# Attention with beacons and a max-out FFN: casts and turns of a pair two to three pairs ahead, loads held by GpSimd memsets

## The chip, the cores and the metric

The kernel runs on one core of one Trainium2 chip. The metric is the device time in microseconds; the median of three runs of the kernel before is 290.99 us (288.12, 290.99 and 295.52). The profile is of one execution. Its span counts from the first to the last instruction of the program; "the profiled run's time" is the device time of that same execution.

Engines are named as in the profile: PE is TensorE (PEld its weight loads), DVE VectorE, ACT ScalarE, POOL GpSimd, SP SyncE, which here only issues DMAs.

## The reference

For 8 batches, 8 heads, 576 tokens, 16 beacons and 64 values a head, attention over beacon keys and causal keys, and after it a feed-forward layer with the maximum of three products:

```
k_all = np.concatenate([beacon_k, k], axis=2)
v_all = np.concatenate([beacon_v, v], axis=2)
scores = scale * np.matmul(q, k_all.transpose(0, 1, 3, 2))
causal[:, Nb:] = np.triu(np.ones((S, S), dtype=bool), k=1)
a = softmax(np.where(causal, -1e9, scores))
x = matmul(a, v_all).transpose(0, 2, 1, 3).reshape(B * S, H * D)
h = np.maximum(np.maximum(x @ w1, x @ w2), x @ w3)
out = h @ w_out
```

x has 4608 rows of 512, h 4608 rows of 768. Inputs and output are float32.

## The kernel before, in words

**Tiles.** Two heads of one batch are a pair: 4 pairs a batch, 32 in all, numbered through. Two pairs are a quad. A pair's q and k come from HBM in float32 into one stage tile "st" of 96 partitions (`load_pair`, line 196), are cast to bf16 into tiles "p" (`cast_pair`, line 265) and turned, so that the head's dimension lies on the partitions, into qT and kT. Pairs from 14 on are turned by a DMA with transpose, two a pair (`cross_piece`, line 375: "turn" in this text); earlier ones by TensorE. There are 8 stage tiles (line 109), 3 buffers for each of the two cast tiles (line 110) and 6 for qT and kT (line 144). V of a batch comes in two pieces, each into a stage tile of the same kind (`load_v`, line 290), and is cast by `cast_v` (line 303) into one of 2 buffers.

**Steps.** The order of the whole program is written out by hand in two lists of steps, `first_steps` (line 897) and `loop_steps` (line 1073). Each step gives its instructions to the engines' queues, and each engine runs its own in that order. The steps that matter:

- `("scores", p, g, ...)` (line 502): the matmuls of group g (of 4) of pair p's scores, and ScalarE's exponential of them (L522).
- `("mask", p, g, "pool")` (line 528): GpSimd zeroes what the causal mask forbids (L541).
- `("values", quad, half, ...)` (line 560): sums and weighted values on TensorE (L582), some 120 small matmuls for the two halves of a quad. "invert" and "multiply" put 1/sum on them (L603, L605, L615) and write x into xT; "cross x" (line 671) copies a part of xT for the other half of TensorE's array.
- `("unit", place)` (line 688): 16 matmuls of x with one of the three weights (L699), and DVE's running maximum (L629, L631). There are 126 units; 18 make one batch's share.
- `("out", n, place)` (line 717): n tiles of h @ w_out (L725); `("store", 1)` sends them out from SP (line 759).
- `("cast", p, "pool", "pool")`: both casts of pair p on GpSimd (L259). `("cross", p, 0)` and `("cross", p, 1)`: the two turns, issued by SP (L378). `("keys", p, "act")`: the beacons' columns of kT (L459).
- `("load", n, gate)` takes the next n loads from the list `loads` (lines 772 to 775) and issues them on SP (L211 for pairs, L276 and L279 for V). With a gate of "pool" or "dve" that engine first writes one column of the stage tile (line 202) or one value (line 294), so that the DMA waits until this engine has come to that place in its own queue. Without a gate the DMA starts as soon as SP reaches it and the tile is free.

SP is one queue: loads, turns and stores leave in the order of the steps.

In a batch of the loop (18 units) stand the scores of 4 pairs, two values steps, four or five tiles of the output, and the casts, turns and loads for later pairs. Below, "unit n" is a place: n units stand before it.

Of the kernel before, what the change touches and what calls it, by code (L numbers as in the profile page):

```python
# [16 lines left out]
def kernel(  # L17
# [15 lines left out]
    B, H, S, D = q.shape  # L33
# [24 lines left out]
    PPB = H // 2  # L58
    PPQ = PPB // n_quad
    NPAIR = B * PPB  # L60
    RING = 3

    B_PE = 4
# [70 lines left out]
    bk32 = const.tile([NB_DMA, H, D], FP32, name="bk32")  # L134
# [43 lines left out]
    def L(fn, *a):  # L178
        return lambda *more: fn(*a, *more)
# [656 lines left out]
    def start_late():  # L836
# [224 lines left out]
        ("load", 1, "pool"),  # L1061
        ("scores", 7, 3, 0),
        ("load", 1),
# [57 lines left out]
        ("cast", 12, "pool", "pool"),  # L1121
        ("load", 1),
        ("load", 1),
        ("scores", 9, 3, 0, 3),
        ("mask", 9, 3, "pool"),
        ("unit", 1),
        ("scores", 9, 1, 0, 0),
        ("mask", 9, 1, "pool"),
        ("unit", 2),
        ("cast", 13, "pool", "pool"),  # L1130
        ("unit", 3),
# [14 lines left out]
        ("cast", 14, "pool", "pool"),  # L1146
        ("cross", 14, 0),
        ("cross", 14, 1),
        ("load", 1),
        ("unit", 2),  # L1150
# [6 lines left out]
        ("cast keys 2", "pool"),  # L1157
        ("load", 1),
# [3 lines left out]
        ("cross keys",),  # L1162
        ("scores", 11, 2, 0, 0),
        ("mask", 11, 2, "pool"),
        ("unit", 1),
        ("scores", 11, 3, 0, 2),
# [4 lines left out]
        ("unit", 1),  # L1171
        ("unit", 2),
        ("cast", 15, "pool", "pool"),
        ("cross", 15, 0),
        ("cross", 15, 1),
        ("load", 1),
# [9 lines left out]
        ("cast", 16, "pool", "pool"),  # L1186
        ("cross", 16, 0),
        ("cross", 16, 1),
        ("load", 1),
# [13 lines left out]
        ("load", 1),  # L1203
        ("cast v", 3, 0, "pool"),
# [3 lines left out]
        ("keys", 14, "act"),  # L1208
# [3 lines left out]
        ("cast v", 3, 1, "pool"),  # L1212
# [6 lines left out]
        ("cast", 17, "pool", "pool"),  # L1219
        ("cross", 17, 0),  # L1220
        ("cross", 17, 1),
        ("load", 1),
# [3 lines left out]
        ("keys", 15, "act"),  # L1226
        ("scores", 13, 3, 0, 3),
        ("mask", 13, 3, "pool"),
        ("unit", 0),
        ("scores", 13, 1, 0, 1),  # L1230
# [5 lines left out]
        ("cast", 18, "pool", "pool"),  # L1236
        ("cross", 18, 0),
        ("cross", 18, 1),
        ("load", 1),
# [3 lines left out]
        ("keys", 16, "act"),  # L1243
# [11 lines left out]
        ("unit", 3),  # L1255
        ("scores", 14, 1, 0, 2),
        ("mask", 14, 1, "pool"),
        ("unit", 0),
        ("cast", 19, "pool", "pool"),
        ("cross", 19, 0),  # L1260
        ("cross", 19, 1),
        ("load", 1),
# [3 lines left out]
        ("keys", 17, "act"),  # L1266
        ("scores", 15, 2, 0, 2),
        ("mask", 15, 2, "pool"),
        ("unit", 0),
        ("scores", 15, 3, 0, 1),  # L1270
# [5 lines left out]
        ("load", 1, "pool"),  # L1276
# [9 lines left out]
        ("cast", 20, "pool", "pool"),  # L1286
        ("cross", 20, 0),
        ("cross", 20, 1),
        ("load", 1),
# [7 lines left out]
        ("load", 1),  # L1297
        ("cast v", 4, 0, "pool"),
# [3 lines left out]
        ("keys", 18, "act"),  # L1302
# [3 lines left out]
        ("cast v", 4, 1, "pool"),  # L1306
# [6 lines left out]
        ("cast", 21, "pool", "pool"),  # L1313
        ("cross", 21, 0),
        ("cross", 21, 1),
        ("load", 1),
# [13 lines left out]
        ("cast", 22, "pool", "pool"),  # L1330
        ("cross", 22, 0),
        ("cross", 22, 1),
        ("load", 1),
# [3 lines left out]
        ("keys", 20, "act"),  # L1337
# [11 lines left out]
        ("unit", 1),  # L1349
        ("scores", 18, 1, 0, 3),  # L1350
        ("mask", 18, 1, "pool"),
        ("unit", 2),
        ("cast", 23, "pool", "pool"),
        ("cross", 23, 0),
        ("cross", 23, 1),
        ("load", 1),
# [3 lines left out]
        ("keys", 21, "act"),  # L1360
        ("scores", 19, 2, 0, 3),
        ("mask", 19, 2, "pool"),
        ("unit", 2),
        ("scores", 19, 3, 0, 0),
# [5 lines left out]
        ("load", 1, "pool"),  # L1370
# [9 lines left out]
        ("cast", 24, "pool", "pool"),  # L1380
        ("cross", 24, 0),
        ("cross", 24, 1),
        ("load", 1),
# [9 lines left out]
        ("load", 1),  # L1393
        ("cast v", 5, 0, "pool"),
# [3 lines left out]
        ("keys", 22, "act"),  # L1398
# [3 lines left out]
        ("cast v", 5, 1, "pool"),  # L1402
# [6 lines left out]
        ("cast", 25, "pool", "pool"),  # L1409
        ("cross", 25, 0),  # L1410
        ("cross", 25, 1),
        ("load", 1),
# [3 lines left out]
        ("keys", 23, "act"),  # L1416
        ("scores", 21, 3, 0, 3),
        ("mask", 21, 3, "pool"),
        ("unit", 2),
        ("scores", 21, 1, 0, 0),  # L1420
# [5 lines left out]
        ("cast", 26, "pool", "pool"),  # L1426
        ("cross", 26, 0),
        ("cross", 26, 1),
        ("load", 1),
# [3 lines left out]
        ("keys", 24, "act"),  # L1433
# [11 lines left out]
        ("unit", 3),  # L1445
        ("scores", 22, 1, 0, 1),
        ("mask", 22, 1, "pool"),
        ("unit", 2),
        ("cast", 27, "pool", "pool"),
        ("cross", 27, 0),  # L1450
        ("cross", 27, 1),
        ("load", 1),
# [3 lines left out]
        ("keys", 25, "act"),  # L1456
        ("scores", 23, 2, 0, 1),
        ("mask", 23, 2, "pool"),
        ("unit", 2),
        ("scores", 23, 3, 0, 0),  # L1460
# [5 lines left out]
        ("load", 1, "pool"),  # L1466
# [9 lines left out]
        ("cast", 28, "pool", "pool"),  # L1476
        ("cross", 28, 0),
        ("cross", 28, 1),
        ("load", 1),
# [7 lines left out]
        ("load", 1),  # L1487
        ("cast v", 6, 0, "pool"),
# [3 lines left out]
        ("keys", 26, "act"),  # L1492
# [3 lines left out]
        ("cast v", 6, 1, "pool"),  # L1496
# [6 lines left out]
        ("cast", 29, "pool", "pool"),  # L1503
        ("cross", 29, 0),
        ("cross", 29, 1),
        ("load", 1),
# [3 lines left out]
        ("keys", 27, "act"),  # L1510
        ("scores", 25, 3, 0, 0),
        ("mask", 25, 3, "pool"),
        ("unit", 1),
        ("scores", 25, 1, 0, 2),
# [5 lines left out]
        ("cast", 30, "pool", "pool"),  # L1520
        ("cross", 30, 0),
        ("cross", 30, 1),
# [3 lines left out]
        ("keys", 28, "act"),  # L1526
# [11 lines left out]
        ("unit", 0),  # L1538
        ("scores", 26, 1, 0, 3),
        ("mask", 26, 1, "pool"),  # L1540
        ("unit", 1),
        ("cast", 31, "pool", "pool"),
        ("cross", 31, 0),
        ("cross", 31, 1),
# [3 lines left out]
        ("keys", 29, "act"),  # L1548
# [17 lines left out]
        ("cross x", 5, 1, 1, "pool"),  # L1566
        ("out", 2, 1),
# [8 lines left out]
        ("cast v", 7, 0, "pool"),  # L1576
# [3 lines left out]
        ("keys", 30, "act"),  # L1580
# [3 lines left out]
        ("cast v", 7, 1, "pool"),  # L1584
# [5 lines left out]
        ("unit", 1),  # L1590
        ("scores", 29, 2, 0, 2),
        ("mask", 29, 2, "pool"),
        ("unit", 0),
        ("keys", 31, "act"),
        ("scores", 29, 3, 0, 3),
        ("mask", 29, 3, "pool"),
        ("unit", 1),
        ("scores", 29, 1, 0, 2),
# [4 lines left out]
        ("unit", 1),  # L1603
        ("scores", 30, 2, 0, 2),
# [106 lines left out]
```

## Time and profile before

| | |
|---|---|
| runs | 288.12, 290.99, 295.52 us; median 290.99 |
| profiled run's own time | 288.71 us |
| its span | 286.9 us |
| granted clock of TensorE | 1.00 |
| moved by DMA | 46.27 MB, 161 GB/s on average |
| SP's queue (q1) | 111888 packets, 39.20 MB |
| instructions' queue (q8) | 40 packets, 0.66 MB |

The program has three stretches: the start up to 57 us, in which the first batches are computed as their data come in; the loop, from "late" at some 57 us to the last scores at some 250 us; and the end, which has only units and output tiles. A row of the table by stretches gives for each engine its busy time and its number of instructions, then the granted clock, the share of the DMA engines' time and GB/s. A row of the timeline has the start, the length, the engine and line, and in square brackets the idle time before it with what ended it. For DMAs on SP the length is the time that SP needed to issue it, not the transfer.

### The profile page before, as it was taken

Reading aid. Unit: us, or ns where it says so; the run is one execution under the profiler, and the core shown is the slowest. Engines: PE = TensorE matmul, PEld = TensorE weight load, DVE = VectorE, ACT = ScalarE, POOL = GpSimd, SP = SyncE. Lnnn points to the kernel's source line nnn. Section 1 sums busy time; section 2 is a strip of 40 time slices with the busy share of each in tenths; the row PEclk is TensorE's granted clock in tenths of the full one; section 3 lists DMA queues with packets and bytes.
Section 4 is the critical chain, followed back from the end, with each engine's and each line's share of the span. In section 5 each row is a group of like instructions: output and inputs, shape, how many; then the busy total and the mean of one; then the engine's idle time right before and its main releaser. Section 6 shows DMA issues by size and latency. Waiting matters only on the chain.

```text
span 286.9 us, 11693 instructions
## 1 busy us (share of the span) xinstructions
PE 275.5 (96%) x5099; PEld 204.3 (71%) x5099; DVE 177.1 (62%) x331; ACT 155.1 (54%) x249; POOL 140.6 (49%) x280
## 2 busy tenths in 40 slices
PE   7999999899899999999999998989999999999995
PEld 6656777667677577876888476866888478867762
DVE  2455878866566665756666565645666565761654
ACT  3886676877363367734765176624765186624000
POOL 4562228898763187626763396616763173400000
PEclk9999999999999999999999999999999999999999
DMA  9999999989999989889999999899999220003004
GB/s 156 177 166 210 219 238 159 244 198 218 231 185 159 148 167 305 133 156 177 192 218 163 158 162 295 138 185 164 242 214 141 78 110 5 2 3 148 2 2 183
DMA packets 118307, 46.27 MB, mean 161 GB/s; under 512 B 107248, under 2 KB 112880, under 8 KB 118256
## 3 DMA queue, kind: packets, MB, share of 16 engines
q1 hardware_dynamic: 111888, 39.20, 72.8%
q0 software_dynamic: 5808, 6.00, 13.3%
q8 instruction: 40, 0.66, 1.1%
q10 hardware_dynamic: 560, 0.33, 0.4%
q14 instruction: 11, 0.09, 0.1%
HBM read 35.13 MB, written 9.44 MB: 155 GB/s over the span
## 4 chain that ended last, share of the span: by engine, by line
PE 87%; DMA 4%; ACT 3%; issue 2%; POOL 1%; DVE 1%; ACTq 0%; POOLq 0%
PE t L699 44%; PE t L725 16%; PE t L582 11%; PE t L513 6%; DMA quad<-in_k_dram 2%; ACT at_sb L522 2%; PE pv L637 2%; DMA bk<-in_beacon_k_dram 2%; PE sc L513 1%; PE sc L637 1%; PE fps L637 1%; PE t L397 1%; POOL at_sb L541 1%; PE wide L582 1%; PE pv L582 1%
## 5 line engine op out<-in xcount | busy, mean ns | idle before, releaser
L699 PE MATMUL t<-xT,w_sb 64*128 64x288 bf16 (+1 forms) x1008 | 130.5, 285 | 0.9 <-issue 0.9
L699 PE MATMUL t<-xC,wC 64*128 64x288 bf16 (+1 forms) x1008 | 130.3, 285 | 0.0
L522 ACT ACTIVATE at_sb<-t 128x992 bf16<-128x992 f32 (+1 forms) x96 | 82.7, 863 | 54.4 <-PE t L513 46.4
L541 POOL TENSOR_SCALAR_AFFINE_SELECT at_sb<-at_sb 128x256 bf16<-128x256 bf16 (+2 forms) x143 | 53.3, 389 | 61.2 <-ACT at_sb L522 46.4
L631 DVE TENSOR_TENSOR hT<-hT,t 128x576 bf16<-128x576 bf16 (+1 forms) x84 | 63.7, 762 | 31.3 <-PE t L699 31.3
L699 PEld LDWEIGHTS <-w_sb 64*128 64x128 bf16 x1008 | 52.7, 94 | 12.8 <-issue 2.1
L699 PEld LDWEIGHTS <-wC 64*128 64x128 bf16 x1008 | 52.7, 94 | 11.3
L725 PE MATMUL t<-w_out_sb,hT 128*128 128x512 bf16 x210 | 46.9, 380 | 0.0
L259 POOL CAST p<-st 96x768 bf16<-96x768 f32 x44 | 35.0, 822 | 8.0 <-DMA qT<-p 7.4
L629 DVE CAST hT<-t 128x576 bf16<-128x576 f32 (+1 forms) x36 | 27.7, 769 | 15.2 <-PE t L699 15.0
L615 DVE TENSOR_TENSOR xT<-t,recip 128x288 bf16<-128x288 f32 (+2 forms) x78 | 23.0, 351 | 22.6 <-ACT recip L605 18.9
L725 PEld LDWEIGHTS <-hT 128*128 128x128 bf16 x210 | 19.9, 98 | 23.3 <-issue 0.2
L680 POOL COPY xC<-xT 64x576 bf16<-64x576 bf16 (+1 forms) x26 | 18.2, 699 | 36.1 <-DVE xT L615 35.9
L513 PE MATMUL t<-qT,kT 64*128 64x288 bf16 (+4 forms) x288 | 33.4, 279 | 0.0
L733 DVE COPY y<-t 128x1024 f32<-128x1024 f32 (+1 forms) x20 | 21.8, 1090 | 17.1 <-PE t L725 16.8
L582 PEld LDWEIGHTS <-v_sb 128*32 128x32 bf16 (+1 forms) x1408 | 24.8, 96 | 5.4 <-issue 4.2
L582 PE MATMUL t<-at_sb,v_sb 128*32 128x96 bf16 (+8 forms) x1144 | 24.0, 228 | 3.2 <-issue 3.2
L513 PEld LDWEIGHTS <-kT 64*128 64x128 bf16 x400 | 18.8, 94 | 10.7 <-issue 6.3
L603 ACT ACTIVATE lnd<-t 128x288 f32<-128x288 f32 x26 | 10.7, 410 | 28.7 <-PE t L582 28.7
L522 ACT ACTIVATE at_sb<-sc 128x736 bf16<-128x736 f32 (+5 forms) x28 | 23.2, 862 | 4.3 <-PE sc L513 4.1
L315 POOL CAST v_sb<-st 128x1536 bf16<-128x1536 f32 (+2 forms) x21 | 18.4, 894 | 0.0
L637 PEld LDWEIGHTS <-w_sb 128*128 128x128 bf16 x144 | 13.1, 98 | 3.3 <-issue 1.4
(125 smaller groups left out, 214.2 us busy)
## 6 DMA issues: line engine op xcount, KB each, us to landing
out_dram<-y SPq DMA_DIRECT2D x15, 512.0 KB, 5.3
st<-in_q_dram SPq DMA_DIRECT2D x24, 288.0 KB, 5.8
st<-in_k_dram SPq DMA_DIRECT2D x24, 288.0 KB, 6.6
st<-in_v_dram SPq DMA_DIRECT2D x24, 256.0 KB, 5.4
w_sb<-in_moe_w_dram POOLq DMA_DIRECT2D x6, 384.0 KB, 8.4
st<-in_v_dram SPq DMA_DIRECT2D x8, 224.0 KB, 4.9
st<-in_v_dram SPq DMA_DIRECT2D x8, 160.0 KB, 5.2
out_dram<-y SPq DMA_DIRECT2D x5, 256.0 KB, 2.7
```

Of the source, the lines that this page charges most:

```text
L259: cast(t16.rearrange("p r h d -> p h r d"), st[0:QP, i * NQ2 : (i + 1) * NQ2].rearrange("p (h r d) -> p h r d", h=2, r=QR),)
L513: nc.tensor.matmul(ps[:, e, off : off + q1 - q0], kT[hs, 128 * t : 128 * t + 128], qT[hs, q0:q1], start=True, stop=True, tile_position=(64 ...
L522: nc.scalar.activation(out=both_heads(p, gi), in_=ps[:, :, 0 : g_width(p, gi)], func=AF.Exp, scale=scale)
L541: nc.gpsimd.affine_select(out=view, in_=view, compare_op=ALU.is_ge, fill=0.0, base=x0, pattern=[[0, 2], [1, hi - lo]], channel_multiplier=-1,)
L582: nc.tensor.matmul(ps[bank][32 * j : 32 * j + 32, lo + q0 - qa : lo + qb - qa], lhsT, at_view(PPQ * quad + j // 2, t, j % 2, q0, qb), star ...
L615: nc.vector.tensor_mul(xT[:, 2 * g + part - 1, c0 + ca : c0 + cb], ps[bank][:, lo : lo + cb - ca], recip[:, ca:cb],)
L629: (by_i or by_dve)(h, ps)
L631: nc.vector.tensor_max(h, h, ps)
L637: nc.tensor.matmul(ps[:, f], w_in[i][:, ct, 128 * (ft + f) : 128 * (ft + f + 1)], xT[:, ct, lo : lo + MID], start=(ct == 0), stop=(ct == n ...
L699: nc.tensor.matmul(ps[:, e], w[own(e), ct, cols], x, start=(ct == 0 and not over), stop=(ct == n_ct - 1 and over), tile_position=(64 * e, 0),)
L725: nc.tensor.matmul(ps[:, u], h_tile(tt + u, ft), w_out_sb[:, ft, :], start=(ft == 0), stop=(ft == n_ft - 1),)
L733: nc.vector.tensor_copy(y[:, 0:n], ps[:, 0:n])
```

## The change

Three things. The list of loads gets another order: the beacons' keys and then, batch by batch, V and the four pairs of the batch after it (before, the pairs came one earlier). Casts, turns and keys of a pair stand later among the steps, so that a pair is turned two to three pairs ahead of its scores instead of four. And the loads, some of which stood together, are spread over the batch, most of them with a memset on GpSimd as gate; the others follow the turns of the same place and have none. The prologue loses two loads (pairs 14 and 15), which move into the loop. Scores, masks, units, values, "out" and "store" keep their order among each other.

Where the steps stand for one batch and for the loads around it ("unit" as above; the same distances return in each batch):

| | before | after |
|---|---|---|
| load of pairs 14, 15 | prologue (gate POOL, none) | units 1, 5 (both POOL) |
| load of V of batch 3, two pieces | 4, 9 (no gates) | 9, 13 (POOL) |
| load of pairs 16, 17, 18, 19 | 4, 12, 17, 18 (no gates) | 16 POOL, 18 none, 20 none, 24 POOL |
| load of V of batch 4 | 23, 27 (no gates) | 27, 30 (POOL) |
| load of pair 20 | 19 (no gate) | 33 (POOL) |
| cast and turns of 14, 15, 16, 17 | 9, 17, 18, 23 | 18, 20, 27, 31 |
| cast and turns of 18, 19, 20, 21 | 27, 31, 36, 41 | 36, 38, 45, 49 |
| first scores of 18, 19, 20, 21 | 44, 49, 54, 58 | the same |
| casts of V of batch 4 | 37, 39 | 41, 43 |

The diff, cut to its core (one batch, from unit 36 on; the other batches are changed alike):

```
-    loads += [L(load_beacons, B_PE, B, bk32)] + load_pairs(16, 17)
+    loads.append(L(load_beacons, B_PE, B, bk32))
     for b in range(3, B):
-        loads += load_v_pieces(b) + load_pairs(PPB * b + 5, min(PPB * b + 9, NPAIR))
+        loads += load_v_pieces(b) + load_pairs(PPB * (b + 1), min(PPB * (b + 2), NPAIR))
...
-        ("load", 1, "pool"),
         ("scores", 7, 3, 0),
-        ("load", 1),
...
         ("cross x", 2, 1, 1, "pool"),
-        ("cast", 20, "pool", "pool"),
-        ("cross", 20, 0),
-        ("cross", 20, 1),
-        ("load", 1),
+        ("cast", 18, "pool", "pool"),
+        ("cross", 18, 0),
+        ("cross", 18, 1),
+        ("load", 1, None),
         ("out", 2, 0),
         ("store", 1),
         ("out", 2, 1),
         ("store", 1),
         ("scores", 16, 0, 0, 3),
         ("mask", 16, 0, "pool"),
         ("unit", 2),
-        ("load", 1),
-        ("cast v", 4, 0, "pool"),
         ("scores", 16, 2, 0, 0),
         ("mask", 16, 2, "pool"),
         ("unit", 3),
-        ("keys", 18, "act"),
+        ("cast", 19, "pool", "pool"),
+        ("cross", 19, 0),
+        ("cross", 19, 1),
+        ("load", 1, None),
+        ("keys", 17, "act"),
         ("scores", 16, 3, 0, 1),
         ("mask", 16, 3, "pool"),
         ("unit", 2),
-        ("cast v", 4, 1, "pool"),
         ("scores", 16, 1, 0, 0),
         ("mask", 16, 1, "pool"),
         ("unit", 3),
         ("scores", 17, 0, 0, 1),
         ("mask", 17, 0, "pool"),
         ("unit", 2),
-        ("cast", 21, "pool", "pool"),
-        ("cross", 21, 0),
-        ("cross", 21, 1),
-        ("load", 1),
+        ("cast v", 4, 0, "pool"),
         ("scores", 17, 2, 0, 0),
         ("mask", 17, 2, "pool"),
         ("unit", 3),
-        ("keys", 19, "act"),
+        ("load", 1, "pool"),
+        ("keys", 18, "act"),
         ("scores", 17, 3, 0, 1),
         ("mask", 17, 3, "pool"),
         ("unit", 2),
+        ("cast v", 4, 1, "pool"),
         ("scores", 17, 1, 0, 0),
         ("mask", 17, 1, "pool"),
         ("unit", 3),
         ("scores", 18, 0, 0, 1),
         ("mask", 18, 0, "pool"),
         ("unit", 2),
-        ("cast", 22, "pool", "pool"),
-        ("cross", 22, 0),
-        ("cross", 22, 1),
-        ("load", 1),
+        ("cast", 20, "pool", "pool"),
+        ("cross", 20, 0),
+        ("cross", 20, 1),
+        ("load", 1, "pool"),
+        ("keys", 19, "act"),
```

More of the change, by code (lines that the diff above doesn't have):

```diff
@@ L1126 @@
         ("unit", 1),
+        ("cast", 12, "pool", "pool"),
+        ("load", 1, "pool"),
         ("scores", 9, 1, 0, 0),
@@ L1129 @@
         ("unit", 2),
+        ("unit", 3),
         ("cast", 13, "pool", "pool"),
-        ("unit", 3),
         ("scores", 10, 0, 0, 1),
@@ L1145 @@
         ("unit", 0),
-        ("cast", 14, "pool", "pool"),
-        ("cross", 14, 0),
-        ("cross", 14, 1),
         ("load", 1),
+        ("load", 1, "pool"),
         ("unit", 2),
@@ L1161 @@
         ("unit", 3),
-        ("cross keys",),
+        ("load", 1, "pool"),
         ("scores", 11, 2, 0, 0),
@@ L1165 @@
         ("unit", 1),
+        ("cast keys 2", "pool"),
         ("scores", 11, 3, 0, 2),
@@ L1171 @@
         ("unit", 1),
+        ("load", 1, "pool"),
         ("unit", 2),
[L1173 to L1176, printed above, removed]
+        ("cross keys",),
         ("unit", 3),
@@ L1185 @@
         ("cross x", 1, 1, 1, "pool"),
[L1186 to L1189, printed above, removed]
+        ("cast", 14, "pool", "pool"),
+        ("cross", 14, 0),
+        ("cross", 14, 1),
+        ("load", 1, None),
         ("pair", 12, "act", "dve", 2),
@@ L1207 @@
         ("unit", 2),
-        ("keys", 14, "act"),
+        ("cast", 15, "pool", "pool"),
+        ("cross", 15, 0),
+        ("cross", 15, 1),
+        ("load", 1, None),
         ("scores", 12, 3, 0, 3),
@@ L1218 @@
         ("unit", 0),
[L1219 to L1222, printed above, removed]
+        ("cast v", 3, 0, "pool"),
         ("scores", 13, 2, 0, 1),
@@ L1225 @@
         ("unit", 2),
-        ("keys", 15, "act"),
+        ("load", 1, "pool"),
+        ("keys", 14, "act"),
         ("scores", 13, 3, 0, 3),
@@ L1229 @@
         ("unit", 0),
+        ("cast v", 3, 1, "pool"),
         ("scores", 13, 1, 0, 1),
@@ L1235 @@
         ("unit", 0),
[L1236 to L1239, printed above, removed]
+        ("cast", 16, "pool", "pool"),
+        ("cross", 16, 0),
+        ("cross", 16, 1),
+        ("load", 1, "pool"),
+        ("keys", 15, "act"),
         ("scores", 14, 2, 0, 1),
@@ L1255 @@
         ("unit", 3),
+        ("load", 1, "pool"),
         ("scores", 14, 1, 0, 2),
@@ L1258 @@
         ("unit", 0),
[L1259 to L1262, printed above, removed]
+        ("cast", 17, "pool", "pool"),
+        ("cross", 17, 0),
+        ("cross", 17, 1),
         ("scores", 15, 0, 0, 1),
@@ L1269 @@
         ("unit", 0),
+        ("load", 1, "pool"),
         ("scores", 15, 3, 0, 1),
@@ L1275 @@
         ("unit", 0),
-        ("load", 1, "pool"),
         ("unit", 1),
@@ L1301 @@
         ("unit", 3),
-        ("keys", 18, "act"),
+        ("cast", 19, "pool", "pool"),
+        ("cross", 19, 0),
+        ("cross", 19, 1),
+        ("load", 1, None),
+        ("keys", 17, "act"),
         ("scores", 16, 3, 0, 1),
@@ L1319 @@
         ("unit", 3),
-        ("keys", 19, "act"),
+        ("load", 1, "pool"),
+        ("keys", 18, "act"),
         ("scores", 17, 3, 0, 1),
@@ L1349 @@
         ("unit", 1),
+        ("load", 1, "pool"),
         ("scores", 18, 1, 0, 3),
@@ L1352 @@
         ("unit", 2),
[L1353 to L1356, printed above, removed]
+        ("cast", 21, "pool", "pool"),
+        ("cross", 21, 0),
+        ("cross", 21, 1),
         ("scores", 19, 0, 0, 0),
@@ L1363 @@
         ("unit", 2),
+        ("load", 1, "pool"),
         ("scores", 19, 3, 0, 0),
@@ L1379 @@
         ("cross x", 3, 1, 1, "pool"),
[L1380 to L1383, printed above, removed]
+        ("cast", 22, "pool", "pool"),
+        ("cross", 22, 0),
+        ("cross", 22, 1),
+        ("load", 1, None),
         ("out", 2, 2),
@@ L1397 @@
         ("unit", 1),
-        ("keys", 22, "act"),
+        ("cast", 23, "pool", "pool"),
+        ("cross", 23, 0),
+        ("cross", 23, 1),
+        ("load", 1, None),
+        ("keys", 21, "act"),
         ("scores", 20, 3, 0, 3),
@@ L1408 @@
         ("unit", 2),
[L1409 to L1412, printed above, removed]
+        ("cast v", 5, 0, "pool"),
         ("scores", 21, 2, 0, 0),
@@ L1415 @@
         ("unit", 1),
-        ("keys", 23, "act"),
+        ("load", 1, "pool"),
+        ("keys", 22, "act"),
         ("scores", 21, 3, 0, 3),
@@ L1419 @@
         ("unit", 2),
+        ("cast v", 5, 1, "pool"),
         ("scores", 21, 1, 0, 0),
@@ L1425 @@
         ("unit", 2),
[L1426 to L1429, printed above, removed]
+        ("cast", 24, "pool", "pool"),
+        ("cross", 24, 0),
+        ("cross", 24, 1),
+        ("load", 1, "pool"),
+        ("keys", 23, "act"),
         ("scores", 22, 2, 0, 0),
@@ L1445 @@
         ("unit", 3),
+        ("load", 1, "pool"),
         ("scores", 22, 1, 0, 1),
@@ L1448 @@
         ("unit", 2),
[L1449 to L1452, printed above, removed]
+        ("cast", 25, "pool", "pool"),
+        ("cross", 25, 0),
+        ("cross", 25, 1),
         ("scores", 23, 0, 0, 0),
@@ L1459 @@
         ("unit", 2),
+        ("load", 1, "pool"),
         ("scores", 23, 3, 0, 0),
@@ L1475 @@
         ("cross x", 4, 1, 1, "pool"),
[L1476 to L1479, printed above, removed]
+        ("cast", 26, "pool", "pool"),
+        ("cross", 26, 0),
+        ("cross", 26, 1),
+        ("load", 1, None),
         ("out", 2, 2),
@@ L1491 @@
         ("unit", 3),
-        ("keys", 26, "act"),
+        ("cast", 27, "pool", "pool"),
+        ("cross", 27, 0),
+        ("cross", 27, 1),
+        ("load", 1, None),
+        ("keys", 25, "act"),
         ("scores", 24, 3, 0, 0),
@@ L1502 @@
         ("unit", 1),
[L1503 to L1506, printed above, removed]
+        ("cast v", 6, 0, "pool"),
         ("scores", 25, 2, 0, 2),
@@ L1509 @@
         ("unit", 3),
-        ("keys", 27, "act"),
+        ("load", 1, "pool"),
+        ("keys", 26, "act"),
         ("scores", 25, 3, 0, 0),
@@ L1513 @@
         ("unit", 1),
+        ("cast v", 6, 1, "pool"),
         ("scores", 25, 1, 0, 2),
@@ L1519 @@
         ("unit", 1),
-        ("cast", 30, "pool", "pool"),
-        ("cross", 30, 0),
-        ("cross", 30, 1),
+        ("cast", 28, "pool", "pool"),
+        ("cross", 28, 0),
+        ("cross", 28, 1),
+        ("load", 1, "pool"),
+        ("keys", 27, "act"),
         ("scores", 26, 2, 0, 2),
@@ L1538 @@
         ("unit", 0),
+        ("load", 1, "pool"),
         ("scores", 26, 1, 0, 3),
@@ L1541 @@
         ("unit", 1),
-        ("cast", 31, "pool", "pool"),
-        ("cross", 31, 0),
-        ("cross", 31, 1),
+        ("cast", 29, "pool", "pool"),
+        ("cross", 29, 0),
+        ("cross", 29, 1),
         ("scores", 27, 0, 0, 2),
@@ L1566 @@
         ("cross x", 5, 1, 1, "pool"),
+        ("cast", 30, "pool", "pool"),
+        ("cross", 30, 0),
+        ("cross", 30, 1),
         ("out", 2, 1),
@@ L1579 @@
         ("unit", 0),
-        ("keys", 30, "act"),
+        ("cast", 31, "pool", "pool"),
+        ("cross", 31, 0),
+        ("cross", 31, 1),
+        ("keys", 29, "act"),
         ("scores", 28, 3, 0, 3),
@@ L1590 @@
         ("unit", 1),
+        ("cast v", 7, 0, "pool"),
         ("scores", 29, 2, 0, 2),
@@ L1597 @@
         ("unit", 1),
+        ("cast v", 7, 1, "pool"),
         ("scores", 29, 1, 0, 2),
```

36 lines of the change are left out of this document (8 added, 28 removed).

## The prediction

> **What bounds the kernel now.** I read the busy table first, then the slices, the stretches by batch, the chain, and last the queues of SP and POOL.
>
> ```profile
> span 286.9 us, 11693 instructions
> PE 275.5 (96%) x5099; PEld 204.3 (71%) x5099; DVE 177.1 (62%) x331; ACT 155.1 (54%) x249; POOL 140.6 (49%) x280
> PEclk9999999999999999999999999999999999999999
> DMA  9999999989999989889999999899999220003004
> q8 instruction: 40, 0.66, 1.1%
> PE 87%; DMA 4%; ACT 3%; issue 2%; POOL 1%; DVE 1%; ACTq 0%; POOLq 0%
> ```
>
> TensorE is busy 96% at the full granted clock; the other engines stand at 49 to 62%. The DMA engines are full up to slice 31 (222 us) and almost idle after it. Where PE loses its 4% decides what a reordering can bring. The table by stretches, cut at the batches, shows it (columns: PE, PEld, DVE, ACT, POOL, clock, DMA share, GB/s):
>
> ```profile
> 0.00:57.00 57.00, 52.00 (x990) 38.59 (x990) 37.04 (x106) 39.31 (x64) 28.97 (x71) 1.00 1.11 196
> 57.00:75.30 18.30, 18.30 (x304) 12.39 (x307) 11.98 (x18) 13.07 (x22) 16.21 (x23) 1.00 1.07 203
> 75.30:94.00 18.70, 17.42 (x434) 13.17 (x433) 11.54 (x20) 8.79 (x15) 8.78 (x18) 1.00 1.02 197
> 94.00:126.40 32.40, 32.40 (x624) 24.27 (x621) 21.01 (x34) 18.62 (x32) 18.51 (x36) 1.00 0.97 180
> 126.40:157.20 30.80, 30.80 (x609) 24.55 (x602) 19.42 (x33) 17.59 (x28) 18.54 (x36) 1.00 1.08 186
> 157.20:191.40 34.20, 32.28 (x607) 23.74 (x607) 20.67 (x35) 17.59 (x28) 19.16 (x37) 1.00 1.14 185
> 191.40:222.20 30.80, 30.80 (x603) 24.41 (x602) 19.02 (x31) 17.59 (x28) 17.88 (x35) 1.00 1.15 194
> 222.20:286.90 64.70, 61.46 (x954) 43.17 (x953) 36.43 (x58) 22.52 (x35) 12.53 (x27) 1.00 0.16 59
> ```
>
> From 57 to 222 us, which is the loop up to its last loads, PE stands still for 1.28 and 1.92 us and nowhere else. The first 57 us lose 5.0, the end 3.2. The chain in order of time names the stops in the loop:
>
> ```profile
> 56.09 0.91 issue
> ...
> 77.11 1.28 issue
> ...
> 94.69 6.48 PE t L725 x30
> ...
> 101.49 0.98 PE t L699 x16
> 102.66 0.98 PE t L699 x16
> ...
> 178.48 0.91 issue
> ...
> 190.22 1.01 issue
> ...
> 240.47 2.29 PE t L582 x111
> ...
> 251.74 2.29 PE t L582 x117
> ```
>
> "Issue" is time in which PE waited for nothing that the profile shows. All four lie in or right behind a "values" step (L582), where some 120 matmuls and their weight loads pass in 2.29 us, so I take them for TensorE's instructions coming in late: instructions have a DMA queue of their own (q8, 40 transfers, 0.66 MB). Together they are 0.91 + 1.28 + 0.91 + 1.01 = 4.11 us. All fall while the DMA engines are full; the two values steps at 240 and 251 us, with idle DMA engines, have none. Of the ten values steps between 75 and 222 us three have one.
>
> **The change, part by part.**
>
> TensorE's list is not touched: every scores, unit, values, pair and out step keeps its place among the others. Its busy time changes by 0; what can change is only its waits.
>
> Memsets. Of the loop's loads 20 are now held by a memset on POOL, 3 were; the prologue loses one. 16 more:
>
> ```profile
> L202 POOL MEMSET st<- x6: 95/98/153, 22.6 to 187.1; 96x1 f32 x6
> ```
>
> 16 x 0.098 = 1.6 us of POOL time, over some 170 us in which POOL is idle for about half. The cover is that idle time; without it, it would cost at most 1.6. The stage tile that a memset writes was freed by a cast that stands earlier on POOL (for pairs 10 and 11 on ScalarE, before the loop's first unit), so the memset waits for nothing new. What waits is SP: nothing behind the held load may pass it. Casts, memsets and the turns that wait for the casts stand in one order on POOL and SP, so a turn is not held by a later load; the stores behind a load get their turn as before or sooner.
>
> Loads later. Pairs 14 and 15 leave the prologue (units 1 and 5 now), V of batch 4 goes from units 23 and 27 to 27 and 30, pair 20 from 19 to 33. From load to cast there remain 9 to 17 units (pair 20: unit 33 to 45, pair 27: 60 to 74), each 0.98 us of PE with its scores 1.17 (102.66 - 101.49), so over 10 us; a landing takes:
>
> ```profile
> DMA to landing us min/median/max: 2.1/5.4/13.5
> ```
>
> The median is covered twice over; the maximum is from a queue that is full. 0.
>
> Casts and turns later. This is what could hurt. One step of the queue as it is:
>
> ```profile
> 129.22 1.59 POOL L259 CAST p<-st 96x768 bf16<-96x768 f32 x2
> ...
> 136.03 1.16 POOL L315 CAST v_sb<-st 128x512 bf16<-128x512 f32 x2
> ...
> 149.45 1.59 POOL L259 CAST p<-st 96x768 bf16<-96x768 f32 x2
> ```
>
> ```profile
> 133.75 2.21 SPq L378 DMA_TRANSPOSE qT<-p  x1
> 136.06 2.26 SPq L378 DMA_TRANSPOSE kT<-p  x1
> ...
> 139.69 1.66 SPq L759 DMA_DIRECT2D out_dram<-y  x2
> ...
> 159.38 1.20 SPq L378 DMA_TRANSPOSE qT<-p  x1
> 160.67 1.22 SPq L378 DMA_TRANSPOSE kT<-p  x1
> ```
>
> Pair 20's cast ended at 130.8, its turn was issued at 133.75; pair 23's ended at 151.0 and its turn went out at 159.38: SP runs 3 to 8.3 us behind POOL. It can, since the turns were wanted far later. The tightest of the new places is the fourth pair of a batch (15, 19, 23, 27): cast after unit 38 in place of 31 for pair 19, wanted at unit 49. Its row of ScalarE, and that of the scores before its cast:
>
> ```profile
> 132.16 2.06 ACT L522 ACTIVATE at_sb<-t 128x992 bf16<-128x992 f32 x2 [4.77 <-PE t L513]
> 149.58 1.00 ACT L522 ACTIVATE at_sb<-t 128x992 bf16<-128x992 f32 x1 [0.47 <-POOL at_sb L541]
> ```
>
> ```profile
> L541 POOL TENSOR_SCALAR_AFFINE_SELECT at_sb<-at_sb 128x256 bf16<-128x256 bf16 (+2 forms) x143 | 53.3, 389 | 61.2 <-ACT at_sb L522 46.4
> ```
>
> The exponentials of scores 16,0 and 16,2 end at 134.2; a mask of 0.39, then the cast of 1.59: done at 136.2. PE wants the result 0.47 before 149.58, at 149.1. So 12.9 us remain for SP's lag and the transfer, which takes:
>
> ```profile
> DMA to landing us min/median/max: 2.9/5.0/6.4
> ```
>
> Ahead of that turn SP holds, since pair 18's cast (130.8), two turns, one pair's load and two stores; the same set took from 133.75 to 141.35 before (the rows above, 7.6 us). So SP is free at 138.4, lag 2.2, landing at 138.4 + 6.4 = 144.8 at worst: 4 us early. Bounds: lag 0 gives 6.5 us to spare; lag 8.3 with 6.4 of transfer is 1.8 us late. I take 2.2, because the held loads shorten the queue; cost 0, cover 4 us, and if it is gone the scores of the fourth pair are late next.
>
> A stall that goes. POOL waited for buffers of the cast, behind a turn:
>
> ```profile
> 101.14 0.82 POOL L259 CAST p<-st 96x768 bf16<-96x768 f32 x1 [4.99 <-DMA qT<-p]
> ```
>
> Pairs 12 and 13 hold two of three buffers there; with only pair 14 cast before them the 4.99 us go. Worth 0: PE was in the output products until 101.17 (94.69 + 6.48, above).
>
> Values of V. The second V cast moves from unit 39 to 43, 1.16 us on POOL where a pair's cast of 1.59 stood before. 0.
>
> The issue stops. Nothing in the trace prices them under a thinner queue: none gone is 0, all four gone is -4.11, and if the new order puts one more full stretch under a values step it is about +1. The batches still move the same bytes in 31 to 33 us, so the engines stay nearly full; only the stretch around 56 and 77 us gets lighter (two pairs' loads moved out). I take one gone, -1.0.
>
> One rule speaks for less. The row: the DMA share is 0.97 to 1.15 in every batch, and ten values steps passed under it with three stops. The Trainium skill, "DMA: Bandwidth & Descriptors", section "Queues, rings and completion order", says that each DMA engine goes round its queues packet by packet, so that a transfer of another queue waits for one packet of each and not for the backlog. By it a shorter SP queue leaves all four stops (0 in place of -1.0); no run here shows yet which holds.
>
> Sum: 288.71 (the profiled run: 286.9 span and 1.8 around it) + 0 + 0 - 1.0 = 287.7. As to the median: the three runs shown have the median 290.99, 2.3 above the profiled one, and reach from 288.12 to 295.52; the changed kernel has the same PE floor and probably the same scatter, so I put half of that distance on: 288.8.
>
> **The rivals.**
> 1. All stops go, and PE runs through: 288.71 - 4.11 = 284.6, 2.2% under the median. For it: none of them after 222 us. Against: seven values steps under full DMA have none, and the DMA stays nearly full. 0.11.
> 2. All stops stay, since the backlog never delayed them: 288.7, with the scatter 289.8. For it: full DMA and no stop in seven steps of ten. 0.20. (By the rule named above it is this one.)
> 3. Slower: the fourth pair's turn comes too late. It takes a lag of SP of over 6.5 us at that place (12.9 - 6.4); 8.3 has been seen, though for a queue that nothing pressed. Then 1.8 us of PE in each of four batches: 288.7 + 7.2 = 295.9; 10 us of lag would make it 288.7 + 4 x 3.5 = 302.7. Against: the queue ahead of it is 7.6 us long and starts 5.4 us before the cast is done. 0.10.
> 4. The change holds nothing: SP is behind POOL anyway, so the memset is done before SP comes to the load, and only the order differs. 288.7 to 289.8, as 2; the lag would stay at 3 to 8 us and rival 3 would be near. 0.12.
>
> **How the numbers follow.** Forecast 0.47; 288.8 us. Its own range is 286 to 291. The range 284.8 to 294.0 reaches to rivals 1 and 2 and over most of the scatter; out of it stay rival 3 (0.10) and a little below. 2% of 290.99, about what this measurement can tell from no change, is 5.8: faster means under 285.2, which is rival 1, 0.11; slower means over 296.8, rival 3 with more lag or bad scatter, 0.09; the same 0.80.
>
> **What would show it.** PE's busy time 275 to 276 us; SP's turns issued within 3 us of their casts; the queue's dense stretch ending at about 235 instead of 222 us, with the DMA digits below 9 here and there before; "issue" two to four times, 2 to 4 us; the 4.99 on POOL gone. Wrong: PE waiting for kT or qT in front of scores of pairs 15, 19, 23 or 27 (rival 3), POOL casts waiting for their loads, or a PE share over 97.5% (rival 1).

## The result and the profile after

| | before | after |
|---|---|---|
| median of 22 runs each, us | 289.54 (287.30 to 295.52) | 288.22 (285.33 to 289.75) |
| ratio of the times | | 0.9948 [0.9927, 0.9969] |
| profiled run: time, span, us | 288.71, 286.9 | 288.61, 286.7 |

The change gains half a per cent, 1.3 us of the median: within 2%, but its interval leaves out 1. Ratios here and below leave out executions over 1.5% longer than the fastest of the same kernel, so they can differ from the quotient of two medians. The two profiled runs lie only 0.1 us apart: the one of before is 0.8 under its median, the one after 0.4 over its own. So the times carry how much was gained, and the traces only where.

From the page of the kernel after: the busy times, the DMA slices, and the group of the casts.

```profile
PE 276.2 (96%) x5099; PEld 204.0 (71%) x5099; DVE 177.2 (62%) x331; ACT 155.1 (54%) x249; POOL 142.2 (50%) x296
...
DMA  8999998999978299999999999996999470003004
...
L259 POOL CAST p<-st 96x768 bf16<-96x768 f32 x44 | 35.1, 824 | 0.3
```

PE has the same 5099 matmuls. The slices of the DMA engines show what the new order does: a hole from the 12th to the 14th slice (79 to 100 us), and more transfers behind the 31st (222 us). The casts wait 0.3 us in all. The table by stretches, with the columns of the prediction's table:

```profile
57.00:75.30 18.30, 18.30 (x309) 12.33 (x301) 12.53 (x19) 13.09 (x22) 16.74 (x27) 1.00 1.04 247
75.30:94.00 18.70, 18.33 (x433) 13.56 (x418) 12.00 (x24) 9.22 (x15) 6.19 (x17) 1.00 0.85 146
...
157.20:191.40 34.20, 31.85 (x605) 23.50 (x604) 19.75 (x32) 17.61 (x28) 18.84 (x39) 1.00 1.21 187
191.40:222.20 30.80, 30.21 (x598) 23.47 (x597) 19.20 (x32) 16.92 (x27) 18.23 (x37) 1.00 1.10 180
222.20:286.90 64.70, 61.28 (x954) 43.13 (x952) 36.26 (x58) 22.47 (x36) 15.60 (x31) 1.00 0.24 71
```

From 57 to 75 us the DMA engines now move 247 GB/s, not 203, and from 75 to 94 us 146, not 197: over both together the rate is about the same (196 for 200), and what leaves first has changed. From 75 to 94 us PE stands for 0.37 us in place of 1.28. The chain in order of time, its stops alone ("issue": PE waits for nothing that the profile shows):

```profile
33.56 0.46 issue
...
56.15 0.30 issue
...
76.56 0.37 issue
...
177.02 1.07 issue
...
188.91 1.28 issue
...
212.84 0.59 issue
```

From 50 us on these are 0.30 + 0.37 + 1.07 + 1.28 + 0.59 = 3.61 us, against 4.11 before. The stop at 77 us has shrunk by 0.9; those at 177 and 189 have grown by 0.4 together, and one at 213 is new. What SP did ahead of the first of them, in the timeline of before (first fence) and after (second):

```profile
64.33 4.80 SPq L211 DMA_DIRECT2D st<-in_q_dram  x1
69.18 1.44 SPq L211 DMA_DIRECT2D st<-in_k_dram  x1
70.93 6.89 SPq L759 DMA_DIRECT2D out_dram<-y  x2
```

```profile
63.14 2.80 SPq L759 DMA_DIRECT2D out_dram<-y  x2
68.83 0.34 SPq L211 DMA_DIRECT2D st<-in_q_dram  x1
```

Before, the loop's first two stores stood on SP behind the loads of pairs 14 and 15 and left at 70.9 us; after, those loads come later and the stores leave at 63.1. That is a side effect of the prologue's part of the change, and the experiments ask whether it is all of it.

### The profile page after: what moved, and what is told of

Its sections match the earlier page's. It is cut to its first block, busy times and chain, and to the rows that moved or that the text cites. A ratio compares the mean times of both kernels' runs of the same rounds, so it can differ in the third digit from the quotient of the medians.

```text
span 286.7 us, 11731 instructions
## 1 busy us (share of the span) xinstructions
PE 276.2 (96%) x5099; PEld 204.0 (71%) x5099; DVE 177.2 (62%) x331; ACT 155.1 (54%) x249; POOL 142.2 (50%) x296
## 2 busy tenths in 40 slices
DMA packets 118307, 46.27 MB, mean 161 GB/s; under 512 B 107248, under 2 KB 112880, under 8 KB 118256
## 4 chain that ended last, share of the span: by engine, by line
PE 90%; ACT 3%; DMA 2%; issue 2%; POOL 1%; DVE 1%; ACTq 0%; POOLq 0%
PE t L699 44%; PE t L725 16%; PE t L582 11%; PE t L513 6%; DMA quad<-in_k_dram 2%; ACT at_sb L522 2%; PE pv L477 2%; PE pv L637 2%; PE sc L513 1%; PE sc L637 1%; PE fps L637 1%; PE t L397 1%; POOL at_sb L541 1%; PE wide L582 1%; PE pv L582 1%
## 5 line engine op out<-in xcount | busy, mean ns | idle before, releaser
L699 PEld LDWEIGHTS <-w_sb 64*128 64x128 bf16 x1008 | 54.1, 94 | 14.1 <-issue 3.2
L699 PEld LDWEIGHTS <-wC 64*128 64x128 bf16 x1008 | 54.1, 94 | 11.7
```

What stands on the lines that cost most here:

```text
L699: nc.tensor.matmul(ps[:, e], w[own(e), ct, cols], x, start=(ct == 0 and not over), stop=(ct == n_ct - 1 and over), tile_position=(64 * e, 0),)
```

## The experiments

The expectations name the theories by letters. A: the gain comes from the prologue, where the loads of pairs 14 and 15 no longer stand ahead of the first stores. B: it comes from the memsets, which hold loads back and thin SP's queue. C: it comes from the later casts and turns. D: the stops are TensorE's instructions arriving late while the DMA engines are full, so they depend on that load and on where a block of instructions ends. For the last one the trace was read further: it has 10228 instructions of TensorE and 40 transfers of 16 KB on q8, which makes 256 instructions a transfer, a block. Counted in order of issue, every large stop of the loop in before and after lies at the same place of a block (remainder 192 to 195 of 256).

**Only the prologue's loads moved** (before, with nothing else of the change).

```
-        ("load", 1, "pool"),
         ("scores", 7, 3, 0),
-        ("load", 1),
...
         ("cast v", 2, 0, "pool"),
+        ("load", 1, "pool"),
         ("scores", 8, 1, 0, 0),
...
         ("load", 1),
         ("load", 1),
+        ("load", 1),
```

> The kernel before with one part of the change alone: the loads of pairs 14 and 15 leave the prologue for units 1 and 2 of the loop; all casts, turns and other loads as before. Theory A (the gain comes from a lighter DMA queue in the first 80 us, so that TensorE's stops at 56 and 77 us shrink from 0.91 and 1.28 us to 0.30 and 0.37): the stops shrink here too, 0.995 of before. Theory B (the gain comes from holding the loads over the loop) and theory C (from the later casts and turns): 1.000, stops at 56 and 77 us as before.

Measured: 287.29 us, ratio 0.9917 [0.9882, 0.9951]. Its stretches and its stops:

```profile
57.00:75.30 18.30, 18.25 (x315) 12.34 (x310) 12.43 (x18) 12.80 (x22) 16.73 (x26) 1.00 1.06 250
75.30:94.00 18.70, 18.64 (x419) 13.69 (x408) 12.37 (x24) 9.22 (x15) 9.34 (x18) 1.00 0.96 166
```

```profile
55.87 0.42 issue
...
176.49 1.07 issue
```

The 250 GB/s are there and the stop at 77 us is not. This small part alone is worth as much as the whole change.

**The change without its memsets** (every load of the loop without a gate).

```
-        ("load", 1, "pool"),
+        ("load", 1),
...
```

> The changed kernel without the loop's memsets: all loads of the loop stand where they stand after the change, but none has a gate. Theory B (holding the loads is what gains): back to 1.000 of before. Theories A and C: as the changed kernel, 0.995, and SP reaches most loads no earlier than the memset would have let them go.

Measured: 287.92 us, 0.9955 [0.9920, 0.9989], about the changed kernel's own ratio. V of batch 3 left SP at 81.69 us against 81.16 with its gate, pair 16 at 87.08 against 87.85; only pair 14 left clearly sooner, at 66.80 for 68.83. At these places the memsets hold little that the order had not already fixed, and B falls.

**The change with pairs 14 and 15 back in the prologue.**

```
+        ("load", 1, "pool"),
         ("scores", 7, 3, 0),
+        ("load", 1),
...
         ("cast v", 2, 0, "pool"),
-        ("load", 1, "pool"),
...
         ("cast", 12, "pool", "pool"),
-        ("load", 1, "pool"),
```

> The changed kernel with pairs 14 and 15 loaded in the prologue again, the rest as changed. Theory A: back to 1.000 of before, stops of about 0.9 and 1.3 us at 56 and 77 us. Theories B and C: 0.995 with those stops small.

Measured: 289.82 us, 1.0006 [0.9967, 1.0045]. SP's timeline, and the chain around the stop:

```profile
70.48 1.54 SPq L211 DMA_DIRECT2D st<-in_k_dram  x1
72.33 6.92 SPq L759 DMA_DIRECT2D out_dram<-y  x2
```

```profile
76.96 1.78 PE t L582 x81
78.73 1.54 issue
80.28 0.70 PE t L582 x37
```

With the stores at 72.3 us the stop is back, after some 80 matmuls of the values step as before, and the gain is gone, though the later casts and turns and all other held loads are in this kernel. A stands: the rest of the change, at the places it has here, is worth nothing that these runs can tell (0.9967 to 1.0045).

**Before, with the two loads right behind the two stores.** This splits A: is it the loads' being ahead of the stores (A1), or their being early at all (A2)?

```
-        ("load", 1, "pool"),
         ("scores", 7, 3, 0),
-        ("load", 1),
...
         ("out", 2, 0),
         ("store", 1),
+        ("load", 2),
         ("pair", 11, "act", "act", 2),
```

> The kernel before with pairs 14 and 15 loaded right behind the two stores of the loop's start instead of ahead of them (no gates), all else as before; they leave SP at about 64 to 70 us, hardly later than before. Theory A1 (the two loads cost because the stores of the first output tiles stand behind them on SP, 70.93 us before and 63.14 after the change, so that reads and writes do not overlap and the DMA moves 203 instead of 250 GB/s from 57 to 75 us): as the prologue change alone, 0.992, and about 250 GB/s in that stretch. Theory A2 (it is their being early that costs): 1.000, the stop at 77 us stays above 0.9 us.

Measured: 287.96 us, 0.9943 [0.9910, 0.9975].

```profile
63.47 3.35 SPq L759 DMA_DIRECT2D out_dram<-y  x2
66.92 1.50 SPq L211 DMA_DIRECT2D st<-in_q_dram  x1
```

```profile
75.66 1.78 PE t L582 x83
77.44 0.21 issue
77.65 0.70 PE t L582 x36
```

The loads go out as early as they can behind the stores and without a gate, and the gain is the same: A1. The records of q8's transfers in the traces show how the order reaches TensorE. For the block that ends at the stop (us; a block is "used up" when its last matmul starts, and these columns and the last are from TensorE's records):

```
kernel                   block before ended   transfer        used up   PE goes on
before                   72.11                75.74 to 77.11  76.91     78.39
14 and 15 in prologue    73.73                77.47 to 78.83  78.53     80.28
after                    71.56                73.82 to 75.35  76.36     76.94
14 and 15 behind stores  72.43                74.93 to 76.29  77.24     77.65
```

The transfer is begun after the block before has ended, takes 1.4 to 1.5 us, and PE goes on 1.3 to 1.6 us after its end. What differs is the wait in front of it: 3.6 and 3.7 us with the loads ahead of the stores, 2.3 and 2.5 without. What else the DMA engines carried there is in the queue's rows of before, 72 to 76 us (first fence), and after (second):

```profile
q0 software_dynamic: 82, 0.36, 40.1%
```

```profile
q0 software_dynamic: 8, 0.02, 2.7%
```

These are GpSimd's copies wC<-w_sb, issued from 65.05 us before and from 64.50 after, in packets of 6 KB that by the trace's records take 0.44 us each there; q1's small ones take 0.03. Before, they are still under way with the stores at that time; after, they are all but done. With 14 and 15 in the prologue again that queue has 45 packets from 74 to 78 us, behind the stores 24 from 72 to 76. Which of the two transfers makes the refill wait was not tried.

**The change with few loads.** Its expectation says which data it leaves out.

```
     def load_pair(p, gate=None):
+        if p >= 16:
+            stage["pair", p] = kept["pair"]
+            return
...
     def load_v(b, piece, gate=None):
+        if b >= 3:
+            stage["v", b, piece] = kept["v", piece]
+            return
```

> The changed kernel without the loads of pairs 16 to 31 and of V of batches 3 to 7 (the casts read the tiles of pair 15 and of batch 2 again; that part of the data is left out); casts, turns, memsets of the other loads and stores stay. Theory D (the stops called issue are TensorE's instruction blocks of 256 that arrive late because the DMA engines are full): the stops at 177, 189 and 213 us (1.07, 1.28, 0.59) go or fall below 0.3 each, the span falls by 2 to 3 us. Rival E (the stops are set by the instruction stream alone and the DMA load has no part): they stay within 0.2 us of what they are.

Measured: 285.51 us, 0.9845 [0.9797, 0.9893], from four runs. The DMA slices, and PE in the stretches that had the late stops:

```profile
DMA  8999998999920251515533281306332450003004
```

```profile
157.20:191.40 34.20, 34.15 (x617) 24.78 (x617) 21.57 (x37) 17.62 (x28) 20.08 (x38) 1.00 0.32 75
191.40:222.20 30.80, 30.75 (x601) 24.45 (x601) 19.50 (x33) 17.61 (x28) 18.65 (x36) 1.00 0.37 75
```

```profile
33.84 0.65 issue
...
76.77 0.61 issue
```

With a DMA share of 0.32 to 0.37 PE runs through; the stops that are left lie where the engines are full. At 174.4 us the block's transfer begins 0.04 us after the block before has ended (1.15 in the changed kernel). So D holds for what makes a stop. The median lies 3.7 us under that of before measured beside it (289.24); rival 1 had put 4.11 on the stops.

**The change with TensorE's list shifted** against the blocks, by 24 instructions fewer (19 longer spare matmuls for 31 at the start) and by 74 more.

```
-        ("busy", 31, 174),
+        ("busy", 19, 284),
```

> The changed kernel with 24 instructions fewer on TensorE before the first data come (19 idle matmuls of 284 columns for 31 of 174), all else the same. Theory D (TensorE's instructions come in blocks of 256, a stop happens where a block is used up in under about 4 us): the stops at 189 and 213 us go or shrink under 0.3, one comes near 143 us, the one at 177 shrinks; in all about 1 us less, 0.991 to 0.996 of before. Rival (stops belong to a place in the work, such as the values step of quad 11): they stay at 177, 189 and 213 us.

Measured: 288.15 us, 0.9948 [0.9916, 0.9979]. Its late stops:

```profile
144.75 0.35 issue
...
178.74 1.48 issue
```

Those at 189 and 213 us are gone, as D has it (though the one at 189 is missing in a second profile of the unshifted kernel too, below), but the one at 178 grew where it should have shrunk: where stops stand was foretold, how long they are was not. Against the changed kernel (0.9948) there is no gain. The other shift:

```
-        spare(ps[:, 0], idle)
+        spare(ps[:, 0], 2 * idle, 160)
...
-        ("busy", 31, 174),
+        ("busy", 46, 117),
```

> The changed kernel with 74 instructions more on TensorE before 30 us (46 idle matmuls of 117 columns for 31 of 174, and those ahead of the first scores cut in halves of 160 columns), all else the same. Theory D: the stops at 177 and 189 us go, others come near 57, 92, 114, 206 and 217 us, 0.5 to 1.5 us each; 1 to 3 us more in all, 0.998 to 1.005 of before. Rival (a place in the work): as the changed kernel, stops at 177, 189 and 213 us.

Measured: 290.31 us, 1.0021 [0.9991, 1.0051], some 2 us over the changed kernel.

```profile
53.84 0.78 issue
...
58.91 1.91 issue
...
117.79 1.09 issue
...
211.36 0.46 issue
...
222.54 0.90 issue
```

None of the old places is left; the stop at 211 us comes 74 instructions of the old list ahead of the one at 213. In all kernels with a shifted list the late stops again lie at remainder 192 to 195 of 256: the block's end decides where a stop is.

**The prologue's part with the shift by 24.** The diff is the two above together.

> The kernel before with the loads of pairs 14 and 15 moved into the loop (the first experiment's edit) and 24 TensorE instructions fewer before the first data. Theories A and D together: the first experiment's 0.992 or up to 0.5 us better, 0.990 to 0.992, the stop at 176 us smaller than 1.07, perhaps one of 0.5 near 143 us. If theory D is wrong: 0.992 with the stop of 1.07 at 176 us.

Measured: 287.66 us, 0.9946 [0.9919, 0.9974]: no better than either part, and outside the 0.990 to 0.992 that was expected. The stops were 0.82, 0.65 and 1.56 us at 57, 145 and 180 us; the last should have been under 1.07. The shift is no way to gain.

**The fourth pairs' turns seven units later** (pairs 19, 23 and 27; the first of the three is shown). This asks how much cover the forecast's riskiest step had.

```
-        ("cast", 19, "pool", "pool"),
-        ("cross", 19, 0),
-        ("cross", 19, 1),
...
         ("scores", 18, 0, 0, 1),
         ("mask", 18, 0, "pool"),
         ("unit", 2),
+        ("cast", 19, "pool", "pool"),
+        ("cross", 19, 0),
+        ("cross", 19, 1),
         ("cast", 20, "pool", "pool"),
```

> The changed kernel with the cast and turns of pairs 19, 23 and 27 seven units later (unit 45 instead of 38, next to those of the pair after). In the changed kernel's profile the turns of pairs 19, 23 and 27 landed 7.4 to 8.8 us before the exponential of their first scores, and the casts would now start about 8.5 us later. Theory F (the cover of the forecast is real and about that large, so the change used up most of it but not all): TensorE now waits for qT or kT by 0.5 to 2.5 us in each of three batches, 1.5 to 7 us in all, 1.000 to 1.019 of before. Rival (other slack hides it, such as SP's queue being shorter there): 0.995 as the changed kernel, no wait of TensorE for a turn.

Measured: 286.90 us, 0.9906 [0.9871, 0.9942]. From the waits of PE (us in all, times, longest):

```profile
PE t L513 <- DMA kT<-p: 0.8, 2, 0.7
```

Scores now wait for the turn, twice, 0.8 us together: the cover is used up. But the wait is small, and the kernel is not slower: the 1.000 to 1.019 and the waits of 1.5 to 7 us in three batches that theory F had did not come.

**The changed kernel a second time**, measured and profiled beside the one above.

> The changed kernel as it is, for a second profile: how far the stops differ between two executions of one program. Theory D with the DMA load deciding their length: the same places (56, 77, 177, 189, 213 us, and 33 us), lengths that differ by some tenths of a microsecond; 0.995 of before.

Measured: 287.77 us, 0.9991 [0.9958, 1.0025], and 0.9957 by the medians of all runs. This interval takes in 1: the ten runs alone do not tell the change from none, and its gain rests on the 22 runs of the result. The stops:

```profile
56.26 1.15 issue
...
177.41 0.86 issue
...
211.66 0.81 issue
```

One and the same program has 0.30 us at 56 in one execution and 1.15 in the other, and 1.28 or nothing at 189. A single stop in a single trace is therefore no evidence. The one at 77 us is another matter: it is 1.28 and 1.54 in the two kernels with the loads ahead of the stores, and at most 0.61 in the kernels without them whose list isn't shifted.

**Those turns six units later.**

```
         ("unit", 3),
+        ("cast", 19, "pool", "pool"),
+        ("cross", 19, 0),
+        ("cross", 19, 1),
         ("scores", 18, 0, 0, 1),
```

> The changed kernel with the cast and turns of pairs 19, 23 and 27 six units later (unit 44; seven units later TensorE waited 0.17 and 0.68 us for two of the turns). If the cover ends where the later turn found it, the waits for kT are gone and the time is as with seven units later or up to 0.9 us less: 0.987 to 0.991 of before. If the seven units gained by chance of the runs alone, this one is as the changed kernel: 0.995 to 0.999.

Measured: 286.80 us, 0.9926 [0.9902, 0.9950], with 0.5 us of waits for kT (0.3 the longest): the waits are not gone, and the time lies between the two ranges expected. Together with the seven-unit kernel this is the fastest that was built on the change with all its data, about 1 us under it in the medians. In both the refill at 174 us began 0.1 and 0.2 us after the block's end, in the two profiles of the changed kernel 1.0 and 1.15. That is one profile of each, and why it is so was not separated. Beside the second measurement of the changed kernel (ten runs, 287.27 to 289.44 us) the seven-unit kernel took 285.49 to 287.65 us in eight, so some 0.9 us over the change are hardly chance; where they come from stays open.

## Why the prediction was right, and where it was not

**TensorE's list, 0.** Held: 276.2 us busy for 275.5. Kernels with the same list showed 275.2 to 277.4, so this difference is scatter.

**Memsets, 1.6 us hidden.** Held: POOL went from 140.6 to 142.2 us, and taking the memsets away changed the time by nothing that shows. The rival "holds nothing", which had 0.12, was nearly right about them; its further condition, SP's lag staying large, was not.

**Loads later, 0.** For the casts it held (0.3 us of waits). But here lies what the prediction missed: "the stores behind a load get their turn as before or sooner" was left without a price. Sooner was 7.8 us at the loop's start (63.14 for 70.93), and it carries the gain.

**Casts and turns later, 0 with 4 us of cover.** Held, with more room. Timelines of the changed kernel: GpSimd's cast of pair 19, SP's two turns, ScalarE's exponential of its first scores.

```profile
133.17 1.59 POOL L259 CAST p<-st 96x768 bf16<-96x768 f32 x2
```

```profile
134.28 2.67 SPq L378 DMA_TRANSPOSE qT<-p  x1
137.05 1.22 SPq L378 DMA_TRANSPOSE kT<-p  x1
```

```profile
148.11 1.00 ACT L522 ACTIVATE at_sb<-t 128x992 bf16<-128x992 f32 x1 [0.47 <-POOL at_sb L541]
```

The casts are done at 134.8, the second turn is issued by 138.3 and had landed at 140.7; PE wanted it 0.47 before 148.11, 147.6. That is 6.9 us early where 4 was the worst case: the second turn left 1.4 us sooner than forecast and landed in 3.7 us, where the maximum of 6.4 was taken, which together outweighs that PE came 1.5 us sooner too. The later turns of the experiment used up just this. The price beyond the cover was too high: the prediction put 1.8 to 3.5 us on each of four batches, and seven units cost 0.8 us in all, in two of three.

**The stall on POOL, 0.** It went, and the row shows why that is worth nothing: the time is now a wait of a mask for its exponential.

```profile
94.82 1.59 POOL L259 CAST p<-st 96x768 bf16<-96x768 f32 x2
101.19 0.74 POOL L541 TENSOR_SCALAR_AFFINE_SELECT at_sb<-at_sb 128x224 bf16<-128x224 bf16 x2 [4.78 <-ACT at_sb L522]
```

**Casts of V, 0.** They never waited.

**The issue stops, -1.0.** The medians moved by -1.3, so the size was right, and instructions arriving late was the right reading. The place was half right: the stretch "around 56 and 77 us" was named, as one that gets lighter. It carries more (247 for 203 GB/s); what matters is the order in it. So "one gone" fits the stop at 77 us (0.9 less), but not for the reason given, and in the two profiles all stops from 50 us on fell by only 0.50. The stop at 56 us lies ahead of the moved loads and varies by itself. That 288.8 came so near to the measured 288.22 is partly luck: 1.1 us of it were put on for the scatter of three runs, and the profiled run after lay 0.4 over its median, not 1.1 under.

**The rule.** The Trainium skill, page "DMA: Bandwidth & Descriptors", section "Queues, rings and completion order", says that each DMA engine goes round its queues packet by packet. By that rule a shorter queue on SP leaves the stops, and the kernel with 14 and 15 back in the prologue agrees: with all the other loads held and spread it had 1.0006, and stops of 1.22, 0.46 and 0.84 us from 180 us on. It does not follow that all four stay: what is under way matters, and with the share at 0.3 the late ones are gone. No run here shows the rounds of an engine packet by packet.

**The signs.** PE's busy time was off by 0.2. The turns mostly left within 3 us of their casts; the first ones of pairs 17, 21, 25 and 29 left 2.7 to 4.6 us after. The last turn left at 233.6 us, near the 235 named, but the queue up to there is not dense: the digits show holes. "Issue" came five times from 50 us on, not two to four, with 3.61 us, inside the 2 to 4.

**The other rivals.** Not all stops went (284.6): even with 15.5 of 46.27 MB left out the median was 285.51. The late turn did not come.

## What to carry to other kernels

When a change moves many things, ask first what now leaves a queue earlier, not only what leaves later: two loads ahead of two stores on SP were worth the 1.3 us, and all the held loads and later turns, at the places this change gave them, nothing that could be told. Where a tuned kernel is bound by one engine at 96%, read its stops one by one, check with a second profile which of them come back, and move only what stands under those. Undoing one side effect in the changed kernel and doing it alone in the old one settles such a question with two runs.

## What the runs showed of the hardware

TensorE's instructions arrive in blocks of 256 (16 KB, 40 transfers for 10228 instructions). At the stops of the loop, a block's transfer began 0.8 to 4.5 us after the block before the current one had been used up, with the DMA engines full (4.5 in the kernel with 74 instructions more); at 174 us it began 1.0 and 1.15 us after in the changed kernel, 0.1 and 0.2 with the later turns, and 0.04 with few loads. A transfer took 0.9 to 2.2 us, and TensorE went on 1.3 to 1.9 us after its end. So a block that is used up sooner than about these three together ends in a stop: those that did had lasted 2.7 to 5.2 us, and the stops were 0.2 to 1.9 us. At 77 and 177 us in the kernels whose list isn't shifted they are blocks with a values step, small matmuls with a weight load each. How long a stop is changes from one execution of the same program to the next (0.30 and 1.15, 1.28 and none).
